# Kernel generation of a four-layer model: inverse deviations on ScalarE, the angle in turns, copies moved from VectorE, values and products exchanged in memory, another order of issue

## The chip, the cores and the metric

The kernel runs on one core of a Trainium2 chip. A core has TensorE (PE, matrix products; its weight loads are listed as PEld), VectorE (DVE, elementwise work and reductions), ScalarE (ACT, elementwise work, copies and functions from a table), GpSimd (POOL), and SyncE (SP), which here issues nearly all DMA transfers. Each engine takes its own instructions in the order in which they are written for it, and waits on semaphores for what other engines produce. The metric is the device time of one execution in microseconds (us).

## The reference, cut to what matters

The model is x = x + A(norm(x)), x = x + B(norm(x)), and both once more with the same weights. x has 2048 rows of 512 bf16 elements.

```
_layernorm: (x - mean) / sqrt(var + 1e-5)

A:  q, k, v = split(x @ wqkv), 32 heads of 16
    each position attends to itself and 7 earlier ones, 2 apart (pos, pos-2, ... pos-14)
    o = softmax(q.k * 16**-0.5, masked where the index is below 0) applied to v;  A = o @ wo

B:  dt = exp(log_dt);  K[d, l] = Re sum_n C[d,n] * exp(dt[d] * A[d,n] * l) * dt[d] * B[d,n],   l = 0 .. 2047
    y = causal convolution of u with K along the rows (by FFT) + u * Dskip
```

A, B and C are complex and given as real and imaginary parts, each 512 x 128. The convolution kernel K doesn't depend on x, so it is made once and serves both B layers.

## The kernel before, in words

There are five stages in time: the generation of K (0 to 117 us), attention layer 0 (to about 202), convolution layer 0 (to about 285), attention layer 1 (to about 378), convolution layer 1. The diff lies in the first, at the borders of the second, and in the order of two memory pools that both attention layers open.

**Generation of K** (`k_gen`, from L884). Its *head* is written out in L905 to L955. The parameters are loaded; PE turns each of them (`transposed`, L924); ACT makes dt = exp(log_dt) (L930); DVE forms dt\*A_im and dt\*A_re from the turned tiles (L939, L940), reduces the angle to one turn (L941 to L944); ACT takes exp of the real part, the sine, the absolute value and, from it, the cosine (L945 to L948); DVE multiplies (L954, L955). That is exp(dt\*A), the first power. Constants of the convolution come from `build_b_consts` (L574), which also hands back a list of small ACT steps (`steps`), a store (`w2_store`, 16 DMAs) and two DVE multiplications (`masks`).

Then powers are squared up eleven times (`square` on ACT, `double` and `differ` on DVE), copied by ACT to bf16 (`power`, `power_neg`), and one plane of each of five powers is duplicated by DMA (`power_copy`). From them DVE builds B_t, the powers for 21 lags (`b_part`), and four tables A_t, each for 32 channels, by doubling (`tables`: a copy of the head c_t at L1098, then five levels of products). PE multiplies tables by B_t (`product`, 16 times), ACT evacuates (`produced`), and `k_store` writes K to DRAM with 24 DMAs. All vector work of this kind shows as L983 in the profile, since one helper records it.

Between these instructions the *front* of attention layer 0 is woven in, for four blocks of 512 rows: load of x (`x_load`), statistics on ACT (`pass_stats`; block 3 by DVE), variance on DVE (`norms`, L1038 to L1055), the inverse deviation (`pow_`, L1059), normalization on ACT (`apply`, L158) or DVE (block 3, L160), turns on PE (L1068), their evacuation (L1071), the projections to keys and queries (L1078, L1083), and the halo copies: the keys of the last rows shifted by one partition (`front_ext`, L247), by DMA for blocks 0 to 2, and by DVE for block 3 (L255). Last come the first three logits products (`first_logits`) and their sums on PE (`la.lsum`).

The order of all this is a string, `ORDERK` (L44): each letter issues the next item of one list. s: square, i: double and differ, b: powers, c: power copies, C and M: c_part and b_part, G: the small ACT steps, g: masks, w: w2_store, a: statistics, l: norms, W: inverse deviation, y and z: normalization on ACT and on DVE, t and e: turn and evacuation, k, q and K, Q: projections and their evacuation, d: loads of x blocks 2 and 3, E: halo by DMA, T and U: tables 0, 2 and tables 1, 3, p and x: product and evacuation, X: first logits products (with the DVE halo before each), Z: their sums, 3: statistics of block 3. Each letter lands on one engine's queue, so the string fixes what stands behind what on every engine.

**Attention layer 0** (`LayerA.core`, L307). For each quarter q and part ft, DVE multiplies queries by eight shifted keys (`mult`, L295), PE sums over the head's 16 elements (`lsum`, L302), ACT takes exp. Projections to values (`v_proj`, L348, evacuated by ACT at L350) go between. After values 14 and 15 a DMA pair shifts values by a partition (L353, L354). Then DVE multiplies attention and values (`pv_mult`, L399), PE sums (L407) and projects (L419). `ev` is a table of further calls at given places: `("v", 1)` is after the second value shift, where all of x is loaded (`x_load`, L1318), `("m", 1, 0)` is ahead of the product of quarter 1, part 0.

Pools in SBUF lie over one another as they are opened: the generation's tiles are freed when its block ends, and the attention's pools take their place. A tile waits for the last reader of whatever lay there. `prp` holds the two product buffers (8 KB per partition each), `big` the values v_ext (30 KB) and the output weights (4 KB).

**Convolution layer 0** (`FftB.run`, with `ORDER0`, L50). Its `late` list holds five calls left over from the attention (the last rows' normalizations, on POOL), one of which is issued after each K letter from the second on.

Of the kernel before, what the change touches and what calls it, by code (L numbers as in the profile page):

```python
# [35 lines left out]
PI_LO = 3.1415920  # L36
# [8 lines left out]
iCsCGiCCCbbsiiMCaasMbiMiaMsCibbiMMaCsbcMTabaiTTibsMTiaMaciTTlbMTlcsiibblTsbTibcTWGiTlbsiGGMGTicM  # L45
GyiaMMMyyyabsGGTaaMGtMMatieMdGMTakaMMqMaMblMlaeaMlMMqkisWMMMaKiMQlywMyMqGyqyMbaMkktTtUQKUapUaUxk
apkKUUUqUxUUpUdUepa3UlTqUleQTkkkKTlUqxTkqK3TkQWqTxk3pTlTxT3yKTlpxpyTkyqkyptTlQkKUqkteqKeTUUTQkkk
WUTUxlkKkUkEKkzUzKpzUUqkEzUxpUKxtUUUUUetpqxekQUkkpxKUUkKkpUxEXkkxpUXKXxqpXXqXQgkpKZZZgxx
# [114 lines left out]
class LayerA:  # L163
# [143 lines left out]
    def core(self, x_sb, u, lnp, ev=None, nprod=0):  # L307
# [14 lines left out]
        with ExitStack() as c2:  # L322
            self.prp = c2.enter_context(tc.tile_pool(name=f"a{l}_prod", bufs=2, reuse_waits="tile"))
            big = c2.enter_context(tc.tile_pool(name=f"a{l}_big", bufs=1, reuse_waits="tile"))
# [3 lines left out]
            self.load_wo(big)  # L328
            wv, wo = self.wv, self.wo
# [15 lines left out]
            def v_proj(a):  # L345
# [5 lines left out]
                if a >= 14:  # L351
                    b = a - 14
                    nc.sync.dma_start(v[1:113, b:14:2, :], v[0:112, 16 + b:30:2, :])  # L353
                    nc.sync.dma_start(v[113:128, b:14:2, :], v[112:127, 16 + b:30:2, :])  # L354
                    event(("v", b))
# [57 lines left out]
            def out_proj(a):  # L413
# [4 lines left out]
                for ftp in range(NDT):  # L418
                    nc.tensor.matmul(pw[:], lhsT=oT[:, ftp, :], rhs=wo[:, ftp, :], start=False, stop=(ftp == NDT - 1))  # L419
# [112 lines left out]
            self.warm(pw, 10, wo[:, 0, :])  # L532
# [41 lines left out]
def build_b_consts(nc, cpool, tmp, w2_dram):  # L574
# [30 lines left out]
    def off_cols(name, rcol, v00, v10, v01, v11):  # L605
        o = tmp.tile([P, 2], F32, name=name)
        nc.vector.tensor_scalar(o[:, 0:1], rcol, float(v10 - v00), float(v00), ALU.mult, ALU.add)
        nc.vector.tensor_scalar(o[:, 1:2], rcol, float(v11 - v01), float(v01), ALU.mult, ALU.add)
        return o

    off = off_cols("w2_off", rik, 2048 * 8, 0, 4096 * 8, 2048 * 8)
    eo = tmp.tile([P, 1], F32, name="w2_eo")
    nc.vector.scalar_tensor_tensor(eo[:], ak, 512.0, d4k, ALU.mult, ALU.mult)
    nc.vector.tensor_tensor(off[:], off[:], eo[:].to_broadcast([P, 2]), ALU.add)
    wps = (("Wp", (4, 12, 0, 8)), ("WpJ", (8, 8, 4, 4)))
    wo = {name: off_cols("off_" + name, rim, *(4096 * o for o in offs)) for name, offs in wps}
    f1t = [tmp.tile([P, P], I32, name=f"f1_t{j}") for j in range(2)]
    qi = tmp.tile([P, EQ, 16, 2], I32, name="w2_qi")
    wt = {name: tmp.tile([P, 2, 16], I32, name="t_" + name) for name, offs in wps}
    ws, w2q = {}, {}  # L620
    sc = 2.0 * math.pi / 65536 * SIN_SHRINK

# [3 lines left out]
    def sine(o, i):  # L626
        nc.scalar.activation(o, i, ACT.Sin, scale=sc)

    def f1_sine(nm, t):
        C[nm] = cpool.tile([P, P], BF16, name=nm)  # L630
        sine(C[nm][:], low16(t[:]))

    def w2_sine():
        w2q[0] = tmp.tile([P, EQ, 32], BF16, name="w2_q", tag="w2_base")
        sine(w2q[0][:].rearrange("p e x -> p (e x)"), low16(qi[:].rearrange("p e m r -> p (e m r)")))

    def w_sine(name):
        ws[name] = cpool.tile([P, 32], F32, name="s_" + name)
        sine(ws[name][:], low16(wt[name][:].rearrange("p r a -> p (r a)")))

    def w_mask(name):
# [8 lines left out]
    def w2_store():  # L650
        for s in range(4):
            for j in range(4):
                nc.sync.dma_start(w2_dram[j::4, s * EQ:(s + 1) * EQ, j * 32:(j + 1) * 32], w2q[0][s::4])
# [787 lines left out]
```

## Time and profile before

| | |
|---|---|
| time, median of 4 runs | 435.51 us (433.08 to 436.96) |
| profiled execution, time | 433.53 us |
| profiled execution, span from first to last instruction | 431.7 us |
| DVE busy | 392.9 us (91%) |
| PE busy | 350.4 us (81%) |
| ACT busy | 322.2 us (75%) |
| POOL busy | 54.9 us (13%) |
| DVE's last product of the head starts | 11.27 us |
| first turn of an x block on PE | 41.52 us |
| product of quarter 0, part 3 starts | 117.26 us |
| first product of attention and values starts | 143.95 us |

The durations behind the steps below are those of one profiled execution. An engine's busy share says how much of the span it works, not whether it sets the end; the waits say who waited for whom, and the chain of work that ended last follows the time back from the last instruction. Names are those of the tiles without their numbers, so that all table work is "A_t" and all products of queries and keys are "prod", "A_pr" or "A2_pr".

### The profile page before, as it was taken

The numbers are of one execution on the slowest core, as the hardware profiler recorded it, in microseconds if no ns is written. First come the engines' busy times: TensorE is split into PE (matmuls) and PEld (weight loads), VectorE is DVE, ScalarE is ACT, GpSimd is POOL, SyncE is SP. The second block draws the span as 40 slices with busy tenths as digits, with TensorE's granted clock in tenths as the row PEclk, the third lists the DMA queues.
The fourth block names the chain that finished last, engine by engine and source line by source line (L and its number), as shares of the span: only waits on it lengthen the run. The fifth ranks groups of instructions, "written<-read, shape, count | busy, mean of one in ns | idle before, by whom it ended". The sixth has DMA issues, their size and how long they took to land.

```text
span 431.7 us, 12684 instructions
## 1 busy us (share of the span) xinstructions
PE 350.4 (81%) x5459; PEld 264.1 (61%) x5502; DVE 392.9 (91%) x549; ACT 322.2 (75%) x544; POOL 54.9 (13%) x46
## 2 busy tenths in 40 slices
PE   2000358998999889999887899999999899997795
PEld 2000117566755667777787798555567777777794
DVE  8999999999999999996989859879999999889874
ACT  6999968676465469987899997864556569689962
POOL 2004040260495000000500000000000020000000
PEclk9999998999999999999999999999999999999999
DMA  8931462132024555482165630860032066225305
GB/s 221 382 102 24 75 71 68 24 70 64 14 46 140 148 177 170 128 348 99 69 241 203 254 124 2 235 205 2 2 92 81 2 256 225 72 88 169 128 27 171
DMA packets 62467, 54.17 MB, mean 125 GB/s; under 512 B 33893, under 2 KB 50890, under 8 KB 61130
## 3 DMA queue, kind: packets, MB, share of 16 engines
q1 hardware_dynamic: 62266, 53.22, 39.9%
q8 instruction: 43, 0.70, 0.6%
q10 hardware_dynamic: 144, 0.13, 0.2%
q14 instruction: 14, 0.11, 0.1%
HBM read 30.28 MB, written 13.24 MB: 101 GB/s over the span
## 4 chain that ended last, share of the span: by engine, by line
PE 40%; DVE 18%; ACT 13%; DMA 5%; SPq 3%; issue 3%; POOL 2%; DVEq 0%; ACTq 0%; POOLq 0%
PE po L407 7%; DVE A_t L983 5%; PE pq L348 4%; DVE prod L295 4%; ACT a1s L726 4%; PE pq L419 4%; PE L L302 3%; PE pp L242 3%; PE pq L185 3%; PE pb L809 3%; PE pb L810 2%; DVE t L784 2%; DVE pav L399 2%; ACT ub L796 2%; PE pk L1135 2%
## 5 line engine op out<-in xcount | busy, mean ns | idle before, releaser
L399 DVE TENSOR_TENSOR pav<-attn,v_ext 128x4096 bf16<-128x4096 bf16 x32 | 72.7, 2281 | 0.0
L295 DVE TENSOR_TENSOR prod<-qT,kT_ext 128x4096 bf16<-128x4096 bf16 x29 | 66.3, 2304 | 0.2
L407 PEld LDWEIGHTS <-pav 128*128 128x128 bf16 x1024 | 58.7, 98 | 11.6 <-DVE pav L399 8.0
L407 PE MATMUL po<-ident,pav 128*128 128x128 bf16 x1024 | 62.5, 219 | 3.5 <-DVE pav L399 3.5
L1068 PE MATMUL pt<-ident,x_blk 128*128 128x128 bf16 x64 | 7.2, 260 | 40.0 <-ACT x_blk L158 38.7
L983 DVE TENSOR_TENSOR A_t<-A_t,pow_t 128x1024 bf16<-128x1024 bf16 (+4 forms) x46 | 38.2, 869 | 0.2
L796 ACT CAST ub<-pb 128x1024 bf16<-128x1024 f32 x32 | 33.0, 1089 | 2.2 <-DVE t L784 2.1
L1078 PE MATMUL pp<-xnT,kT_ext 128*128 128x512 bf16 x87 | 25.9, 421 | 10.7 <-ACT xnT L1071 8.3
L350 ACT CAST v_ext<-pq 128x512 bf16<-128x512 f32 x32 | 18.7, 586 | 20.4 <-PE pq L348 16.5
L809 PE MATMUL pb<-Wp,t 128*128 128x128 bf16 x256 | 30.1, 219 | 2.6 <-ACT ub L796 2.4
L302 PEld LDWEIGHTS <-prod 128*128 128x128 bf16 x928 | 27.0, 96 | 8.3 <-DVE prod L295 3.0
L744 PE MATMUL pb<-a1s,w_sb 128*128 128x64 bf16 x768 | 27.1, 193 | 5.7 <-ACT ub L796 3.5
L348 PE MATMUL pq<-wv,xnT 128*128 128x512 bf16 x118 | 30.2, 379 | 1.2 <-ACT v_ext L350 0.7
L1068 PEld LDWEIGHTS <-x_blk 128*128 128x128 bf16 x64 | 5.1, 116 | 42.6 <-ACT x_blk L158 40.8
L726 ACT CAST a1s<-pb 128x1024 bf16<-128x1024 f32 x30 | 29.3, 1077 | 1.3 <-PE pb L737 1.3
L410 ACT CAST oT<-po 128x512 bf16<-128x512 f32 x32 | 18.5, 579 | 15.7 <-PE po L407 15.6
L810 PE MATMUL pb<-WpJ,t 128*128 128x128 bf16 x256 | 30.1, 219 | 0.0
L419 PE MATMUL pq<-wop,oT 128*128 128x512 bf16 x110 | 29.3, 379 | 0.9
L744 PEld LDWEIGHTS <-w_sb 128*128 128x128 bf16 x768 | 24.7, 98 | 8.1 <-issue 7.0
L1059 POOL TENSOR_TENSOR ln_rstd<-ln_rstd,ln_mh 128x4 f32<-128x4 f32 x4 | 20.3, 5079 | 72.2 <-DVE ln_rstd L1054 49.2
L302 PE MATMUL L<-ind,prod 128*128 128x8 bf16 x928 | 27.5, 166 | 0.6 <-DVE prod L295 0.4
L726 DVE CAST a1s<-pb 128x1024 bf16<-128x1024 f32 x18 | 21.5, 1219 | 6.2 <-PE pb L737 5.9
(226 smaller groups left out, 873.3 us busy)
## 6 DMA issues: line engine op xcount, KB each, us to landing
w_sb<-w_dram SPq DMA_DIRECT2D x8, 1024.0 KB, 8.0
w_dram<-w_zero SPq DMA_DIRECT2D x1, 4096.0 KB, 14.5
kf_ring<-kf_dram SPq DMA_DIRECT2D x13, 256.0 KB, 3.7
kf_ring<-kf_dram SPq DMA_DIRECT2D x26, 128.0 KB, 3.6
v_ext<-v_ext SPq DMA_DIRECT2D x4, 784.0 KB, 6.1
x_blk<-in_A_x_dram SPq DMA_DIRECT2D x4, 512.0 KB
kT_ext<-in_A_wqkv_dram SPq DMA_DIRECT2D x4, 512.0 KB, 5.3
x_sb<-in_A_x_dram SPq DMA_DIRECT2D x4, 512.0 KB, 6.6
```

Source lines behind the costliest of these rows:

```text
L295: nc.vector.tensor_tensor(pr, self.qT[q][:, ft].unsqueeze(1).to_broadcast([P, W, 4, P]), kap, ALU.mult)
L302: self.nc.tensor.matmul(L[:, al, w, ft * 8:(ft + 1) * 8], lhsT=pr[:, w, al, :], rhs=self.c["ind8"][:], start=(ft == 0 and w == 0 and al % ...
L348: nc.tensor.matmul(pp[:], lhsT=xnT[:, dt, a * P:(a + 1) * P], rhs=wv[:, dt, :], start=(dt == 0), stop=(dt == NDT - 1))
L399: nc.vector.tensor_tensor(pv[:], attn[:, n % 4].unsqueeze(2).to_broadcast([P, W, DH, H]), vap, ALU.mult)
L407: nc.tensor.matmul(po[:, ft, :], lhsT=pvf[:, w, ft * P:(ft + 1) * P], rhs=ident[:], start=(w == 0 and ft == 0), stop=(w == W - 1), skip_gr ...
L419: nc.tensor.matmul(pw[:], lhsT=oT[:, ftp, :], rhs=wo[:, ftp, :], start=False, stop=(ftp == NDT - 1))
L726: (self.nc.scalar.copy if eng == "act" else self.nc.vector.tensor_copy)(dst, src)
L744: nc.tensor.matmul(p2[:, j, :], lhsT=self.w2[:, ec * EC + j, :], rhs=a1s[:, ec * EC + j, :], start=True, stop=True)
L796: nc.scalar.copy(ub[:], p2)
L809: nc.tensor.matmul(p3[:, j, :], lhsT=t1[:, dql, :], rhs=wp_r, start=True, stop=False)
L810: nc.tensor.matmul(p3[:, j, :], lhsT=t2[:, dql, :], rhs=wpj_r, start=False, stop=True)
L983: return lambda: nc.vector.tensor_tensor(*args)
```

## The change

1. *Head.* The loads of A_re and A_im change places. The angle is formed in turns: one DVE operation multiplies the turned A_im by 1/(2 pi) and dt, one adds the rounding constant, one takes it off and subtracts, one takes the larger of the turn and its negative. ACT's sine and cosine take 2 pi as their scale; ACT's absolute value, the clamp and one subtraction are gone. dt is written without reordering, and its readers reorder. Two memsets of B_t move from DVE to POOL, and what `build_b_consts` does with small offsets moves behind the angle (`rest`).
2. *Inverse deviations.* POOL's power and DVE's addition of the epsilon give way to ACT's Ln and Exp. The table set that holds both is loaded ahead of the first; the load in `ev` at `("m", 1, 0)` is gone.
3. *Table heads.* The copy of c_t is a letter of its own for tables 1 to 3 (H), on ACT.
4. *Halos.* Of block 3, parts 0 to 2 are copied by ACT (letter o).
5. *Masks.* They move from the end of the generation on DVE to POOL, as a sixth call of convolution layer 0's `late`.
6. *Memory.* `big` is opened ahead of `prp`, in both attention layers. In layer 0 the output weights are loaded after the first value shift, and x block 0 there too; x blocks 1 to 3 after the second.
7. *Order.* `ORDERK` is another string.

```diff
 ORDERK = """
-iCsCGiCCCbbsiiMCaasMbiMiaMsCibbiMMaCsbcMTabaiTTibsMTiaMaciTTlbMTlcsiibblTsbTibcTWGiTlbsiGGMGTicM
-GyiaMMMyyyabsGGTaaMGtMMatieMdGMTakaMMqMaMblMlaeaMlMMqkisWMMMaKiMQlywMyMqGyqyMbaMkktTtUQKUapUaUxk
-apkKUUUqUxUUpUdUepa3UlTqUleQTkkkKTlUqxTkqK3TkQWqTxk3pTlTxT3yKTlpxpyTkyqkyptTlQkKUqkteqKeTUUTQkkk
-WUTUxlkKkUkEKkzUzKpzUUqkEzUxpUKxtUUUUUetpqxekQUkkpxKUUkKkpUxEXkkxpUXKXxqpXXqXQgkpKZZZgxx
+sibCCiGCsiCbGCiMisibsbGcCiCMibabcsMMCMTMGiiMTGMaTbaisiTMbbcTTsiaTGbibsTTaiiaTbbbcMsTGaiGMaMMiGMb
+lMlaMGsGWiiaMalbMyyyyTMMaaiaMtMMweMtaMMMMedTaqcMMMslMkMaqlQkiqWKMbMqMlkyHyQTkyUkUkyKTtUqtKUUppaU
+qaUaUUqUxaUqaQakapxUelQekdUlpUkWKkKHxkqTlT3Tky3qxKTT3pT3pTQylyqxTkWqylxQpTkKtpzzTqzeTkqHtkxQeKUU
+zktkKkUEETkeUUktKTkkUkKTUUeKkkpkxpKUxkpUEUxUKkqUxUUUUpqoUkpoxKXUQxoUkpkKXZpxXxpxZZ
 """
...
         with ExitStack() as c2:
+            big = c2.enter_context(tc.tile_pool(name=f"a{l}_big", bufs=1, reuse_waits="tile"))
             self.prp = c2.enter_context(tc.tile_pool(name=f"a{l}_prod", bufs=2, reuse_waits="tile"))
-            big = c2.enter_context(tc.tile_pool(name=f"a{l}_big", bufs=1, reuse_waits="tile"))
...
-            self.load_wo(big)
-            wv, wo = self.wv, self.wo
+            wv = self.wv
+            if l:
+                self.load_wo(big)
...
                     nc.sync.dma_start(v[113:128, b:14:2, :], v[112:127, 16 + b:30:2, :])
+                    if b + l == 0:
+                        self.load_wo(big)
                     event(("v", b))
...
-            nc.vector.tensor_tensor(C[name][:], ws[name][:].unsqueeze(2).to_broadcast([P, 32, 4]),
-                                dmask_m.unsqueeze(1).to_broadcast([P, 32, 4]), ALU.mult)
+            nc.gpsimd.tensor_tensor(C[name][:], ws[name][:].unsqueeze(2).to_broadcast([P, 32, 4]),
+                                    dmask_m.unsqueeze(1).to_broadcast([P, 32, 4]), ALU.mult)
...
-        for name in ("A_im", "A_re", "B_re", "B_im", "C_re", "C_im"):
+        for name in ("A_re", "A_im", "B_re", "B_im", "C_re", "C_im"):
...
-        nc.vector.memset(Bt[:, 0, :, 0, :], 1.0)
-        nc.vector.memset(Bt[:, 1, :, 0, :], 0.0)
+        nc.gpsimd.memset(Bt[:, 0, :, 0, :], 1.0)
+        nc.gpsimd.memset(Bt[:, 1, :, 0, :], 0.0)
...
-        nc.scalar.activation(nat(dtb[:]), ldt[:].rearrange("p g q -> p q g"), ACT.Exp)
+        nc.scalar.activation(dtb[:], ldt[:].rearrange("p g q -> p (g q)"), ACT.Exp)
+        dtv = dtb[:].rearrange("p (g q) -> p q g", g=4)
...
-        nc.vector.tensor_tensor(nat(a_im), transposed("A_im"), nat(dtb[:]), ALU.mult)
-        nc.vector.tensor_tensor(nat(a_re), transposed("A_re"), nat(dtb[:]), ALU.mult)
-        nc.vector.tensor_scalar(t1[:], a_im, 1.0 / TWO_PI, MAGIC, ALU.mult, ALU.add)
-        nc.vector.tensor_scalar(t1[:], t1[:], MAGIC, None, ALU.subtract)
-        nc.vector.scalar_tensor_tensor(a_im, t1[:], -TWO_PI, a_im, ALU.mult, ALU.add)
-        nc.vector.tensor_scalar(a_im, a_im, PI_LO, -PI_LO, ALU.min, ALU.max)
+        nc.vector.tensor_tensor(nat(a_re), transposed("A_re"), dtv, ALU.mult)
         nc.scalar.activation(a_re, a_re, ACT.Exp)
-        nc.scalar.activation(sn, a_im, ACT.Sin, scale=-1.0)
-        nc.scalar.activation(t2[:], a_im, ACT.Abs)
-        nc.scalar.activation(cs, t2[:], ACT.Sin, bias=math.pi / 2 * (1 - 4e-7), scale=-1.0)
+        nc.vector.scalar_tensor_tensor(nat(turn), transposed("A_im"), 1.0 / TWO_PI, dtv, ALU.mult, ALU.mult)
+        nc.vector.tensor_scalar(t1[:], turn, MAGIC, None, ALU.add)
+        nc.vector.scalar_tensor_tensor(turn, t1[:], MAGIC, turn, ALU.subtract, ALU.subtract)
+        nc.vector.scalar_tensor_tensor(t2[:], turn, -1.0, turn, ALU.mult, ALU.max)
+        nc.scalar.activation(sn, turn, ACT.Sin, scale=TURN)
+        nc.scalar.activation(cs, t2[:], ACT.Sin, bias=math.pi / 2 * (1 - 4e-7), scale=-TURN)
+        steps, w2_store = rest()
...
-                yield lambda: nc.vector.tensor_scalar(rstd[:], var, EPS, None, ALU.add)
                 yield lambda: nc.vector.scalar_tensor_tensor(nb[:], mean, ms, rstd[:], ALU.mult, ALU.mult)
...
-        def pow_(b):
+        def inv_std(b):
             r = ln[b][0]
-            nc.gpsimd.tensor_tensor(r[:], r[:], lnst["mh"][:, 0:4], ALU.pow)
+            if b == 0:
+                nc.scalar.preload_act_table_set(EXP_LN)
+            nc.scalar.activation(r[:], lvar[b], ACT.Ln, bias=EPS)
+            nc.scalar.activation(r[:], r[:], ACT.Exp, scale=-0.5)
...
-            yield lambda: nc.vector.tensor_copy(A[:, :, :, 0, :], c0[:, :, c * CH * 4:(c + 1) * CH * 4].rearrange("p r (q g) -> p r q g", g=4))
+            (nc.scalar.copy if c else nc.vector.tensor_copy)(
+                A[:, :, :, 0, :], c0[:, :, c * CH * 4:(c + 1) * CH * 4].rearrange("p r (q g) -> p r q g", g=4))
...
             for ft in range(3):
-                yield lambda: la.front_ext(3, "dve", ft)
                 yield lambda: mult(ft)
...
-        ev = {("v", 1): [x_load], ("o", 1): [lambda: k_half_load(0)], ("o", 2): [G(gs, 0)], 
-              ("m", 1, 0): [lambda: nc.scalar.preload_act_table_set(EXP_LN)],
+        ev = {("v", 0): [lambda: x_load((0,))], ("v", 1): [lambda: x_load((1, 2, 3))], ("o", 1): [lambda: k_half_load(0)], ("o", 2): [G(gs, 0)], 
...
         late = la.core(x_sb, u, lnp, ev, 3)
+    late.append(C["masks"])
```

## The prediction

> **What bounds the kernel now.** I read the per-engine totals first, then busy time by stretch, then the waits, the chain that ended last, and the timeline of the stretch that the diff touches. Nearly all of the diff lies in the first of five stages, the generation of the convolution kernel. The table by stretch (engine busy time of each stretch, clock, DMA share, GB/s):
>
> ```profile
> 12.00:40.00 28.00, 0.00 (x0) 0.00 (x0) 27.06 (x50) 27.15 (x44) 4.86 (x1) 1.00 0.52 179
> 40.00:70.00 30.00, 14.19 (x80) 7.76 (x83) 28.92 (x48) 25.74 (x56) 5.07 (x1) 0.94 0.43 62
> 70.00:96.00 26.00, 24.64 (x323) 16.68 (x326) 25.14 (x41) 19.71 (x33) 10.32 (x2) 1.00 0.23 54
> 96.00:115.00 19.00, 17.21 (x296) 13.45 (x299) 18.66 (x27) 10.91 (x17) 1.23 (x4) 1.00 0.16 40
> 115.00:135.00 20.00, 19.04 (x290) 11.50 (x293) 19.84 (x16) 10.51 (x18) 20.00 (x14) 1.00 0.23 55
> ...
> 160.00:185.00 25.00, 24.59 (x352) 19.35 (x354) 24.59 (x24) 23.29 (x48) 1.01 (x1) 1.00 0.53 160
> ```
>
> The columns after the length are PE, PEld, DVE, ACT, POOL. From 12 us to 185 us VectorE (DVE) is 96 to 99% busy, through the generation (to 117 us) and the first attention layer (to 190). So a DVE microsecond saved in the generation is worth one, until another engine ends last. Where DVE is idle (the waits, total, times, longest):
>
> ```profile
> DVE ln_nb L1055 <- POOL ln_rstd L1059: 2.7, 3, 0.9
> DVE sq_z L954 <- ACT ws L946: 0.7, 1, 0.7
> DVE sq_z L955 <- ACT ws L948: 0.5, 1, 0.5
> ```
>
> and the chain that ended last passes the third of these POOL waits into TensorE:
>
> ```profile
> 88.78 7.31 POOL ln_rstd L1059
> ...
> 99.50 0.90 PE pt L1068 x13
> ```
>
> Four numbers per partition raised to -0.5 take 7.31 us on GpSimd; then DVE normalizes block 3, PE turns it and has no gap worth a word until 117. The stretch ends so on DVE, ACT and PE:
>
> ```profile
> 116.07 0.28 DVE L643 TENSOR_TENSOR Wp<-s_Wp,aux 128x128 bf16<-128x128 f32 x1
> 116.28 0.69 DVE L643 TENSOR_TENSOR WpJ<-s_WpJ,aux 128x128 bf16<-128x128 f32 x1
> 116.89 0.28 DVE L255 COPY kT_ext<-kT_ext 128x508 bf16<-128x508 bf16 x1
> 117.26 4.72 DVE L295 TENSOR_TENSOR prod<-qT,kT_ext 128x4096 bf16<-128x4096 bf16 x2
> ```
> ```profile
> 118.10 1.07 ACT L350 CAST v_ext<-pq 128x512 bf16<-128x512 f32 x2 [3.62 <-PE L L302]
> ```
> ```profile
> 117.07 0.94 PE L302 MATMUL L<-ind,A_pr 128*128 128x8 bf16 x32
> ```
>
> The first value eviction waits 3.62 us for the third logits sum, because its tile lies over that product's buffer.
>
> **What the Trainium skill says.** "SBUF — State Buffer", section "SBUF: two separate sides": DVE and GpSimd share a port pair under an exclusive lock. The trace agrees: the same 4-element power takes 3.09 to 7.30 us beside a full DVE, 1.01 us once at 174. "ScalarE: Activation LUTs", "What ACT_TABLE_LOAD costs": 1283 ns plus a drain of 1380. The trace has the 1.28 us (at 8.10) but the next activation starts 0.05 after it, so I price 1.3. "Table sets: the hidden batching unit" of the same page: exp and ln lie in one set; at 121 to 131 us one load serves Exp, Ln, Exp, so it agrees. The first of these sections also prices an ACT copy at 186 ns + 0.833 per element, 93 overlapped: 0.31 us for 256 elements, 0.52 for 508 (estimates; 512-element copies here follow at 0.48).
>
> **The change, part by part** (start-to-start times, since DVE instructions overlap by some 0.08).
>
> *Head.* DVE ends it at 11.27 + 0.69 = 11.96. After: eight small w2 offset operations (4.75 to 5.46) and two B_t memsets (5.52 to 6.28) no longer stand ahead of the first product. It can start when the first transpose, done at 5.55, is seen: 5.65, not 6.19. It is now the A_re product, so its Exp ends by 6.95 and the Sin table by 8.25. The angle in turns costs DVE 0.60 + 0.45 + 0.70 + 0.65 to 8.6, the turn itself ready at 7.95. Sine 8.25 to 8.8, cosine 8.8 to 9.4, with no ACT Abs (0.61) between and no clamp (0.43). DVE has meanwhile done the eight offsets (0.6), and its two last products end at 9.75 and 10.4. Gain 1.55; bounds 0.8 (memsets on POOL delaying DVE) to 1.8.
>
> *Off DVE.* Four rstd adds (L1054) at 0.07: 0.28. Three table head copies (L1098) 0.27 + 0.13 + 0.14 = 0.54. Three halo copies (L255, parts 0 to 2) 0.20 + 0.32 + 0.37 = 0.89. Two masks, 116.07 to 116.89: 0.82. Sum 2.53. The masks go to GpSimd behind its last normalizations in the convolution stage, where POOL works 6.0 of 40 us and the inverse products need them some 30 us later: nothing, or about 1 us if that cover is gone.
>
> *The POOL waits* at 38.6, 61.8 and 95.2: 0.91 + 0.91 + 0.90 = 2.72, gone. In their place ACT does Ln and Exp, 0.19 + 0.21 seen at 187.7, with a handover to and from DVE, and DVE has 0.6 to 2 us of other products ordered in between. One table load (1.28) comes before the first; the load at 121.26 goes, where ACT idles half the time, so neither ends last.
>
> *New order.* I laid both order strings out and added each letter's duration along its queue. DVE carries 101.8 us before and 99.5 after, ACT 83.8 and 88.9, PE 48.6 twice. Check on before: 12.0 + 101.8 + 2.7 = 116.5, seen 116.9. ACT after ends near 10.4 + 88.9 = 99.3 plus waits, eleven short of DVE, so it can't bound the sum, only single steps. The tightest: the 16 w2 stores, 11.48 us of SP issue, now stand ahead of the load of x block 2 and of the fifth power copy. They can start when their sine is done (some 30 us of ACT work: 40.7), end at 52.2, the load goes at 52.6 (before 45.88), just when its buffer is free, and lands about 56.5. ACT reaches its statistics at 57.2. The copy lands by 57, its reader comes at 62. Cost 0.4, bounds 0 and 3.
>
> *Value pool below the products.* Summing tile sizes from the bottom, the product buffers leave the power tables (free early) and now lie over the second and third first-logits products; values lie over the first two. So value evictions wait for the second sum, not the third, and the product of part 3 waits for the third sum. Queued behind it on DVE is all of the attention; PE waits for that. The product ends, the sum takes 0.94, DVE has only 0.28 of its own: 0.85 of wait if PE is up to date, 1.8 if it is 1.0 late as at 117.07, none if the buffer falls elsewhere. I take 1.0. The output weights' four loads (3.3 us of SP) move behind the first value shift, and x block 0 ahead of the second: SP idled 137.0 to 144.0 there, so the 4.2 us hide; uncovered they would delay the second shift by at most that. PE's 0.6 wait for x_sb at 152 goes, DVE never saw it.
>
> **Sum.** 1.55 + 2.53 + 2.72 = 6.8 saved, 1.0 + 0.4 given back: **5.4 us**. Attention follows DVE without a gap to 190, and later stages follow attention, so it carries. Span 431.7 becomes 426.3, the profiled execution 433.53 becomes 428.1. The median of the runs shown is 2.0 above that execution, so I forecast 435.51 - 5.4 = **430.1**.
>
> **Rivals.** (a) *Handovers take the place of the POOL waits*: ACT gained 5.1 us of work, in a string where DVE and ACT run within a microsecond of each other up to the 50th microsecond of work, and half of that lands on DVE. For it: squares, powers, table heads and Ln/Exp now all share ACT's queue. Against: ACT idles for 17 of 105 us. 435.5 - 2.8 = 432.7. (b) *Nothing is given back*: 435.5 - 6.8 = 428.7; the buffer falls elsewhere and x arrives in time. (c) *Slower, by SP order*: the w2 stores write 64-byte rows and hold the DMA engines at 0.62 to 0.81; if block 2 lands behind them 14 us after issue, ACT stalls about 10, and through the second inverse deviation DVE loses about 8.6: 438.7. It turns the result from a landing at 63.5 on. Against it: the stores themselves landed 2.7 to 3.5 us after issue, and the x load took 3.5.
>
> **Chances.** About 1% (4.4 us) is what a measurement can tell from no change. Forecast and (b) together, gains above 4.4: 0.61. (a), gains of 0 to 4.4: 0.30. (c) 0.09, of which 0.02 end within 1%. Faster 0.61, same 0.32, slower 0.07. The low end is (b) less the 2 us by which single runs fall around their median, 426.7, the high end no gain at all, 435.5, with half a microsecond on it.
>
> **What would show it.** DVE's two head products end near 10.4. No wait of DVE for POOL before 170, and ACT's Ln/Exp without a wait of DVE over 0.3 behind them. The fourth product of the first tile starts at about 112, preceded by about 1 us of waiting for L; the first pav at about 138.5 (143.95). After that the same gaps as before. I am wrong if DVE waits for ACT in 40 to 80 us, if the statistics of block 2 wait for their load, or if the attention, starting earlier, ends later than 5 us before 202.

## The result and the profile after

The changed kernel takes 432.67 us (median of 34 runs, 430.21 to 435.76) where the kernel before, run beside it, takes 435.00 (53 runs, 433.08 to 438.00). The ratio is 0.9948, with a 95% interval of 0.9933 to 0.9962: a gain of 2.3 us, clear of noise, but less than half of the 5.4 that were forecast. The profiled execution took 432.41 us, its span is 430.6, only 1.1 below that of before. Up to the first convolution stage it is 2.55 ahead, at 320 us 2.98, at 381 us 1.50. The granted clock was 0.83 from 330 to 340 us, where before has 1.00, and 0.3 is lost there; of the rest, lost between 354 and 381 us at a clock of 1.00 in both, 0.6 is a wait of DVE for ACT's rs at 360 us, and what remains is not explained.

| start of | before | forecast | after |
|---|---|---|---|
| end of DVE's last product of the head | 11.96 | 10.4 | 11.85 |
| end of the third first-logits product | 116.07 | | 112.42 |
| fourth product of the first tile | 117.26 | 112 | 114.94 |
| its wait for the sum L | none | 1.0 | 2.07 |
| first product of attention and values (pav) | 143.95 | 138.5 | 141.40 |
| third pav | 151.69 | | 149.14 |
| DVE's first evacuation of the convolution stage | 203.42 | | 200.87 |

The gain is there at the fourth product (2.32 us) and stays through the first attention layer: what decides it lies before 115 us. The table by stretch of the kernel after (PE, PEld, DVE, ACT, POOL busy, clock, DMA share, GB/s):

```profile
12.00:40.00 28.00, 0.00 (x0) 0.00 (x0) 28.00 (x47) 26.61 (x43) 0.00 (x0) 1.00 0.52 177
40.00:70.00 30.00, 14.79 (x117) 8.25 (x120) 29.74 (x50) 28.98 (x62) 3.79 (x2) 1.00 0.45 72
70.00:96.00 26.00, 24.16 (x305) 16.22 (x309) 25.93 (x44) 23.72 (x44) 0.00 (x0) 1.00 0.24 50
96.00:115.00 19.00, 17.80 (x352) 14.29 (x353) 16.79 (x18) 10.52 (x17) 3.36 (x6) 1.00 0.18 43
115.00:135.00 20.00, 18.66 (x253) 10.53 (x254) 19.93 (x13) 9.48 (x17) 17.72 (x11) 1.00 0.34 83
```

Up to 96 us DVE has 0.33 us of idle time in 84 (before: 2.9). The POOL waits are gone and nothing has come in their place. In the fourth stretch it idles 2.2 of 19. DVE's waits name the new one, and the one at the head:

```profile
DVE prod L295 <- PE L L302: 2.1, 1, 2.1
...
DVE sq_z L947 <- PE pt L933: 0.6, 1, 0.6
```

The timeline of DVE (start, length, what; in brackets the idle time ahead of it) at the head, and where the attention begins:

```profile
5.92 1.03 DVE L947 TENSOR_TENSOR sq_z<-pt,dt_bf 128x512 f32<-128x512 bf16 x1 [0.62 <-PE pt L933]
6.87 1.04 DVE L949 SCALAR_TENSOR_TENSOR ws<-pt,dt_bf 128x512 f32<-128x512 bf16 x1
...
11.16 0.69 DVE L962 TENSOR_TENSOR sq_z<-sq_z,ws 128x512 f32<-128x512 f32 x1
...
112.42 0.45 DVE L255 COPY kT_ext<-kT_ext 128x508 bf16<-128x508 bf16 x1
114.94 4.49 DVE L295 TENSOR_TENSOR prod<-qT,kT_ext 128x4096 bf16<-128x4096 bf16 x2 [2.07 <-PE L L302]
```

The two products with dt take 1.03 and 1.04 us; before, they took 0.63 and 0.68, with the same tile sizes and types:

```profile
6.19 0.63 DVE L939 TENSOR_TENSOR ws<-pt,dt_bf 128x512 f32<-128x512 bf16 x1
6.74 0.68 DVE L940 TENSOR_TENSOR sq_z<-pt,dt_bf 128x512 f32<-128x512 bf16 x1
```

And PE's timeline where the attention begins:

```profile
111.36 0.96 PE L302 MATMUL L<-ind,A_pr 128*128 128x8 bf16 x32
112.23 1.89 PE L349 MATMUL pq<-wv,xnT 128*128 128x512 bf16 x7
113.96 0.94 PE L302 MATMUL L<-ind,A_pr 128*128 128x8 bf16 x32
```

and before:

```profile
114.53 0.82 PE L348 MATMUL pq<-wv,xnT 128*128 128x512 bf16 x2
115.19 0.94 PE L302 MATMUL L<-ind,A_pr 128*128 128x8 bf16 x32
116.00 1.24 PE L348 MATMUL pq<-wv,xnT 128*128 128x512 bf16 x5
```

The third product ends at 112.42, but its sum starts at 113.96: PE is in value projections, which lie between the second and the third sum. Before, three such matmuls lay ahead of the second sum and five ahead of the third (the trace lacks the record of one of the three, and here that of one of eight), and that sum started 1.0 after its product's end (117.07 and 116.07); here all eight lie ahead of the third, and it is 1.54 late. The string doesn't show this: in both strings the second and the third sum stand side by side (ZZ), and the attention issues the value projections later; in both traces they run between the sums.

### The profile page after: what moved, and what is told of

Same layout as the page of the kernel before. It is cut to its first block, busy times and chain, and to the rows that moved or that the text cites. A ratio compares the mean times of both kernels' runs of the same rounds, so it can differ in the third digit from the quotient of the medians.

```text
span 430.6 us, 12686 instructions
## 1 busy us (share of the span) xinstructions
PE 349.6 (81%) x5459; PEld 263.9 (61%) x5502; DVE 392.1 (91%) x534; ACT 325.9 (76%) x557; POOL 39.1 (9%) x46
## 4 chain that ended last, share of the span: by engine, by line
PE 46%; DVE 16%; ACT 13%; DMA 4%; issue 4%; SPq 1%; ACTq 0%; DVEq 0%
PE po L410 8%; DVE prod L295 5%; PE pk L1150 5%; DVE pav L402 5%; ACT a1s L733 4%; PE pq L349 4%; PE pq L422 4%; PE pp L1088 4%; PE L L302 3%; PE pp L242 3%; PE pq L185 3%; PE pb L816 3%; PE pb L817 2%; ACT ub L803 2%; DVE t L791 2%
## 5 line engine op out<-in xcount | busy, mean ns | idle before, releaser
L410 PEld LDWEIGHTS <-pav 128*128 128x128 bf16 x1024 | 60.2, 99 | 12.0 <-DVE pav L402 8.1
L410 PE MATMUL po<-ident,pav 128*128 128x128 bf16 x1024 | 64.0, 222 | 4.1 <-DVE pav L402 4.0
L1078 PE MATMUL pt<-ident,x_blk 128*128 128x128 bf16 x64 | 6.3, 241 | 43.4 <-ACT x_blk L158 43.4
L817 PEld LDWEIGHTS <-t 128*128 128x128 bf16 x256 | 25.0, 98 | 3.0 <-issue 1.9
```

The costliest lines, as they stand in the source:

```text
L410: nc.tensor.matmul(po[:, ft, :], lhsT=pvf[:, w, ft * P:(ft + 1) * P], rhs=ident[:], start=(w == 0 and ft == 0), stop=(w == W - 1), skip_gr ...
L817: nc.tensor.matmul(p3[:, j, :], lhsT=t2[:, dql, :], rhs=wpj_r, start=False, stop=True)
```

## The experiments

All times are medians of 6 to 34 executions (six in experiments 1, 5, 6, 8 and 11), each beside runs of the kernel before on the same chip. "Fourth product" and "third pav" are the places of the table above, "head ends" is the end of DVE's last product of the head; these three are from one trace each. With the new head, this end scatters from trace to trace: PE's first transpose, which waits for the load of A_re, starts at 4.89 to 5.20 in the ten traces that have this head, and DVE's first product of the head at 5.62 to 5.92. The kernel after has the latest of the ten, so up to 0.3 us of a difference to it is not the work of the edit. In experiment 2, where the edit doesn't touch the head, it starts so:

```profile
5.65 1.03 DVE L950 TENSOR_TENSOR sq_z<-pt,dt_bf 128x512 f32<-128x512 bf16 x1 [0.35 <-PE pt L936]
```

| edit | time, ratio (95% interval) | head ends | fourth product | third pav |
|---|---|---|---|---|
| after | 432.67, 0.9948 (0.9933, 0.9962) | 11.85 | 114.94 | 149.14 |
| after, dt in natural order | 431.62, 0.9902 (0.9866, 0.9939) | 11.04 | 113.42 | 147.62 |
| after, pools of layer 0 as before | 432.72, 0.9934 (0.9910, 0.9959) | 11.57 | 112.77 | 148.62 |
| after, products moved up by a pad | 432.80, 0.9933 (0.9912, 0.9955) | 11.73 | 112.83 | 148.38 |
| after, power on POOL again | 436.79, 1.0029 (1.0002, 1.0057) | 11.73 | 119.37 | 153.58 |
| after, dt and pad | 430.82, 0.9895 (0.9850, 0.9940) | 11.12 | 111.83 | 147.38 |
| after, old order | 443.83, 1.0191 (1.0147, 1.0235) | 11.55 | 126.05 | 162.36 |
| after, copies on DVE again | 434.42, 0.9974 (0.9956, 0.9992) | 11.54 | 115.17 | 149.38 |
| before, inverse deviations on ACT | 444.53, 1.0198 (1.0151, 1.0245) | 11.97 | 121.16 | 161.68 |
| after, old order, common table named | 437.02, 1.0066 (1.0042, 1.0090) | 11.59 | 119.46 | 153.85 |
| before, the same, common table named | 435.85, 1.0015 (0.9998, 1.0031) | 11.97 | 117.85 | 152.86 |
| after, dt and pad, index work on ACT | 428.92, 0.9873 (0.9839, 0.9907) | 10.87 | 111.40 | 145.09 |
| before, pools exchanged | 435.35, 1.0015 (0.9996, 1.0033) | 11.97 | 118.08 | 152.28 |

**1. dt in natural order.** ACT's exponential writes dt in the order of its readers again, as before the change.

```diff
-        nc.scalar.activation(dtb[:], ldt[:].rearrange("p g q -> p (g q)"), ACT.Exp)
-        dtv = dtb[:].rearrange("p (g q) -> p q g", g=4)
+        nc.scalar.activation(nat(dtb[:]), ldt[:].rearrange("p g q -> p q g"), ACT.Exp)
+        dtv = nat(dtb[:])
...
-                yield tt(nat(c0[:, q]), nat(cb), dtv, ALU.mult)
+                yield tt(c0[:, q], cb, dtb[:], ALU.mult)
```

> The changed kernel with dt stored as before: ScalarE writes it reordered, so that its four readers on VectorE read it in sequence (the two products of the head, the two c_t products). Theory A (the new layout of dt made each of the four 0.36 to 0.41 us longer: 1.03 and 1.04 for 0.63 and 0.68 in the head, 1.04 for 0.69 at c_t): all four fall back to 0.63 to 0.69, dt itself takes 1.07 on ScalarE instead of 0.63 but is ready at about 5.65, before the first product at 5.92; the fourth product of the first tile starts 1.4 us earlier, at about 113.5, and the time is 1.4 us below that of the changed kernel, about 431.2 (ratio to before 0.9915). Rival B (the head is set by ScalarE's table load and sines, or the generation's end by TensorE): the products are shorter, the end moves by less than 0.5 us (ratio 0.994 to 0.995).

The products fall to 0.69 and 0.68, the head ends at 11.04, and the fourth product and the attention behind it come 1.52 us earlier, 0.10 of it because the head's first product starts sooner:

```profile
5.82 0.69 DVE L947 TENSOR_TENSOR sq_z<-pt,dt_bf 128x512 f32<-128x512 bf16 x1 [0.87 <-PE pt L933]
```

By the ratios the time is 2.0 us below that of the changed kernel, but the intervals overlap; the trace decides, for A. DVE's group of the two c_t products, of the kernel after and of this one:

```profile
L990 DVE TENSOR_TENSOR c_t<-ws,dt_bf 128x512 bf16<-128x512 f32 x2 | 2.1, 1044 | 0.0
```
```profile
L990 DVE TENSOR_TENSOR c_t<-ws,dt_bf 128x512 bf16<-128x512 f32 x2 | 1.4, 684 | 0.0
```

So four DVE instructions paid 0.35 us each for reading dt at a stride of 256 bytes. ACT's exponential, which reordered in their place, takes 1.08 us against 0.63, and DVE waits for PE's first transpose in either case: the 0.45 that ACT saved shortened nothing.

**2. Pools of layer 0 as before**: products below the values again, in layer 0 alone.

```diff
+            if not l:
+                self.prp = c2.enter_context(tc.tile_pool(name=f"a{l}_prod", bufs=2, reuse_waits="tile"))
             big = c2.enter_context(tc.tile_pool(name=f"a{l}_big", bufs=1, reuse_waits="tile"))
-            self.prp = c2.enter_context(tc.tile_pool(name=f"a{l}_prod", bufs=2, reuse_waits="tile"))
+            if l:
+                self.prp = c2.enter_context(tc.tile_pool(name=f"a{l}_prod", bufs=2, reuse_waits="tile"))
```

> The changed kernel with the product buffers below the values again, in attention layer 0 alone. Theory A (the 2.07 us wait of the fourth product for the third logits sum is a pure loss, VectorE sets the end): the wait is gone, that product starts at about 112.9 and all that follows comes 2.0 us earlier, about 430.7 (ratio 0.990). Rival B (behind it stands the chain of the values: value evictions now wait for the third sum at 114.9 instead of the second at 112.3, the second value shift, which landed at 148.1 ahead of the third attention product at 149.1, comes later): the product starts at 112.9, but the third attention product waits for the shift and starts no earlier than 148.5; gain 0 to 0.6 us (ratio 0.993 to 0.995).

The wait for L is gone and the fourth product comes 2.17 us earlier, 0.28 of it from the earlier head. But the value evictions now wait for the third sum, PE waits for them, the next reduction waits for L:

```profile
115.33 1.89 PE L352 MATMUL pq<-wv,xnT 128*128 128x512 bf16 x8 [0.72 <-ACT v_ext L354]
118.49 1.23 DVE L366 TENSOR_REDUCE mx<-L 128x128 bf16<-128x1024 f32 x1 [1.02 <-PE L L285]
```

At the third pav 0.52 is left, 0.24 without the head. B by its numbers, but not by its shift: the third pav doesn't wait; the time is lost ahead of it.

**3. A pad**: values stay at the bottom, and the products lie behind the small tiles and a pad of 2.25 KB, clear of the third first-logits product (layer 0 alone).

```diff
             big = c2.enter_context(tc.tile_pool(name=f"a{l}_big", bufs=1, reuse_waits="tile"))
-            self.prp = c2.enter_context(...)
+            if l:
+                self.prp = c2.enter_context(...)
...
             wk = c2.enter_context(tc.tile_pool(name=f"a{l}_wk", bufs=2, reuse_waits="tile"))
+            if not l:
+                pad = c2.enter_context(tc.tile_pool(name="a0_pad", bufs=1, reuse_waits="tile"))
+                pad.tile([P, 1152], BF16, name="pad")
+                self.prp = c2.enter_context(...)
```

> The changed kernel with the product buffers of attention layer 0 opened above the small work tiles and 2.3 KB of padding, so that they lie over a table of the last products (read to 111.3) and over no first-logits product; the values stay where the change put them. Theory A (VectorE sets the end): no wait for the third sum, the fourth product at about 112.9, everything 2.0 us earlier, about 430.7 (ratio 0.990). Rival B (value chain): value evictions are as early as in the changed kernel, so the shift lands at about 148.1 as there and the third attention product can't start before about 148.2: gain 0.9 us at most, about 431.8 (ratio 0.992 to 0.993).

Now neither waits, yet of 2.11 us at the fourth product 0.76 are left at the third pav (0.64 without the earlier head), and nothing sure is seen in the time (by the ratios 0.65 us, with intervals that overlap). The gain is B's, but again no pav waits for the shift. The timelines show where the rest goes. POOL makes index tables (L683, L684 of the kernel after) from 111 us on. In the kernel after, two of its eight multiplications fall into DVE's 2.07 us of idle time and take 1.39 us:

```profile
112.70 1.39 POOL L684 TENSOR_SCALAR g_i<-g_i,aux 128x512 int32<-128x512 int32 x2
...
115.11 5.47 POOL L684 TENSOR_SCALAR g_i<-g_i,aux 128x512 int32<-128x512 int32 x2
```

and with the pad:

```profile
112.58 5.53 POOL L689 TENSOR_SCALAR g_i<-g_i,aux 128x512 int32<-128x512 int32 x2
112.83 4.80 DVE L295 TENSOR_TENSOR prod<-qT,kT_ext 128x4096 bf16<-128x4096 bf16 x2
136.07 0.83 DVE L384 TENSOR_TENSOR s<-ex 128x512 bf16<-128x512 bf16 x1
```

With the pad DVE is busy there, each pair takes 5.3 to 5.6, POOL ends at 137.46 instead of 132.72, and beside it DVE's product takes 4.80 for 4.49 and the second tile's sums 0.83 and 0.66 for 0.41 and 0.29. The idle time had paid for POOL's work; without it, DVE pays (experiment 11 takes that work away). The prediction cited the lock on the shared port (the Trainium skill, "SBUF — State Buffer", section "SBUF: two separate sides") for a power that DVE lengthens; by that section, when a DVE operation with two SBUF inputs meets a GpSimd one that reads SBUF, whichever starts first blocks the other. Here DVE's instructions lengthen, by 0.31 to 0.42 us, which agrees in kind; no run tells the lock from another cause.

**4. The power on POOL again**, with DVE's addition of the epsilon, at the new places.

```diff
-            nc.scalar.activation(r[:], lvar[b], ACT.Ln, bias=EPS)
-            nc.scalar.activation(r[:], r[:], ACT.Exp, scale=-0.5)
+            nc.vector.tensor_scalar(r[:], lvar[b], EPS, None, ALU.add)
+            nc.gpsimd.tensor_tensor(r[:], r[:], lnst["mh"][:, 0:4], ALU.pow)
```

> The changed kernel with the inverse deviations on GpSimd again (VectorE adds the epsilon where the letter W stands, GpSimd raises to -0.5). Theory A (a GpSimd power ends only once VectorE stops, so each costs VectorE a wait of about 0.9 us as the three in the kernel before, plus 0.07 for the addition): four waits, the fourth product of the first tile 3.5 to 4 us later than in the changed kernel, about 118.7, time about 436.4 (ratio 1.003). Rival B (the waits were covered elsewhere, other engines were late anyway): less than 1.5 us later (ratio below 0.998).

```profile
DVE ln_nb L1062 <- POOL ln_rstd L1069: 3.6, 4, 1.2
...
DVE A_t L990 <- ACT A_t L1109: 0.3, 1, 0.3
```

A: the waits are back, four of them, and 4.43 us at the fourth product (4.55 without the earlier head). 3.6 + 0.3 of waits and 0.3 of additions account for 4.2 of it. In this order, taking the power off POOL is worth its waits in full.

**5. dt and pad together.**

> The changed kernel with both mends at once: dt written in the natural order again, and in layer 0 the value pool at the bottom but the product buffers moved up by a pad, clear of the third first-logits product. Theory A (both losses are on VectorE's path and add): the fourth product starts at about 111.4, with no wait for L of more than 0.3; the third pav at about 146.9 (147.6 with dt alone, less 0.76 that the pad alone gave); time 0.8 us below dt alone, 430.8. Theory B (GpSimd's index generation, which sits beside VectorE from 111 us on, takes the pad's gain back, as with the pad alone): the fourth product at 111.4 too, but VectorE's short sums before attn and the products beside GpSimd grow by 1.5 us or more in all, the third pav at 147.3 or later, time as with dt alone, 431.6.

The fourth product is at 111.83, the third pav at 147.38, 0.24 before that of dt alone: by the trace most of the pad's gain is taken back as in experiment 3 (product 4.80, sums 0.83 and 0.66, and a halo copy of 0.69 for 0.45). The time, 430.82, is 0.8 below dt alone, as A has it, but the ratios differ by 0.0007 and their intervals overlap; the trace decides, for B.

**6. The new kernel in the old order.** The order string of before, without its two mask letters and its four epsilon letters; table heads and halos on ACT stand where DVE's copies stood.

> The changed kernel with the order string of before (its mask letters and its four epsilon letters left out, each moved table head and halo copy at the place where it stood). Theory A (the new order moves VectorE little by itself, the POOL waits went because the power left GpSimd): VectorE waits for ScalarE at Ln/Exp or at table heads by less than 1 us in all, the fourth product at 114 to 116, time within 1 us of the changed kernel, 431.7 to 433.7. Theory B (ScalarE has 5 us more in front of VectorE, and the old order has no room for it): VectorE waits for ScalarE by 2 to 5 us in all between 12 and 112 us, the fourth product at 117 or later, time 434.5 or more.

By the ratios 10.6 us slower than the new order, far past B. DVE waits 3.0 for a table head and 2.3 for Ln and Exp before 112 us, then 3.2 for the halo copy and 3.4 for L. ACT's timeline shows a cause that neither theory named:

```profile
96.57 1.28 ACT L1068 ACT_TABLE_LOAD   x1
97.86 0.20 ACT L1068 ACTIVATE ln_rstd<-ln_ag 128x4 f32<-128x4 f32 x1
98.09 1.28 ACT L1069 ACT_TABLE_LOAD   x1
99.38 0.20 ACT L1069 ACTIVATE ln_rstd<-ln_rstd 128x4 f32<-128x4 f32 x1
```

In the whole run ACT loads 19 tables, where before and after load 5. The kernel names the set that has both Exp and Ln once, ahead of the first inverse deviation. In the old order sines come after that (at 48.77 and 66.72 us); they load their own table, and from then on each Ln and each Exp loads one of its own, in the attention of layer 0 too (six loads, beside L384 and L386). The Trainium skill, "ScalarE: Activation LUTs", section "Table sets: the hidden batching unit", counts Ln and then Exp as one load, since one set has both. Here that held only where that set was already the active one.

**7. Copies on DVE again**: table heads 1 to 3 and the three halos; the masks too, at their new, late place.

```diff
-            (nc.scalar.copy if c else nc.vector.tensor_copy)(
+            nc.vector.tensor_copy(
...
-            nc.gpsimd.tensor_tensor(C[name][:], ws[name]...
+            nc.vector.tensor_tensor(C[name][:], ws[name]...
...
-... o=calls(lambda ft: la.front_ext(3, "act", ft), (0,), (1,), (2,)) ...
+... o=calls(lambda ft: la.front_ext(3, "dve", ft), (0,), (1,), (2,)) ...
```

> The changed kernel with table heads and halo copies back on VectorE (and the two masks on VectorE at their new, late place). Theory A (what leaves VectorE in the generation shortens the run by its own length): 0.54 + 0.89 = 1.43 us later at the fourth product, 116.4, the wait for L stays at 2.1, time 434.1. Theory B (the wait for L absorbs it, since it ends by TensorE's value projections, which don't depend on these copies): the wait shrinks to 0.6 to 1.0, the fourth product within 0.4 of 114.94, time as the changed kernel, 432.7 within 0.5.

```profile
115.17 4.49 DVE L295 TENSOR_TENSOR prod<-qT,kT_ext 128x4096 bf16<-128x4096 bf16 x2 [1.50 <-PE L L302]
```

The third product ends 0.97 later, the wait shrinks by 0.57, and the fourth product is 0.23 later; without the earlier head of this execution (0.31) it would be some 0.54. So B's mechanism is there, the wait ends by PE's queue and takes up part of the copies, but less of them than B has it. The time is A's (434.42; by the ratios 1.1 us above the changed kernel), in part for another reason: the masks on DVE at 207 us (0.71 and 0.28) delay the convolution stage by another 0.8, from 0.56 at its start to 1.34 at 233 us.

**8. The kernel before with the inverse deviations on ACT**, and nothing else.

```diff
-                yield lambda: nc.vector.tensor_scalar(rstd[:], var, EPS, None, ALU.add)
+                lvar[b] = var
+                yield lambda: None
...
-            nc.gpsimd.tensor_tensor(r[:], r[:], lnst["mh"][:, 0:4], ALU.pow)
+            if b == 0:
+                nc.scalar.preload_act_table_set(EXP_LN)
+            nc.scalar.activation(r[:], lvar[b], ACT.Ln, bias=EPS)
+            nc.scalar.activation(r[:], r[:], ACT.Exp, scale=-0.5)
...
-              ("m", 1, 0): [lambda: nc.scalar.preload_act_table_set(EXP_LN)],
```

> The kernel before with only the inverse deviations moved: Ln and Exp on ScalarE in the place of VectorE's epsilon add and GpSimd's power, the order string as it was. Theory A (the forecast's terms): the three POOL waits, 2.72, and four adds, 0.28, go: the fourth product at 114.3 (117.26 before), time 3.0 us below before, ratio 0.993. Theory B (handovers take their place): VectorE waits for ScalarE's Ln/Exp by half of that, the fourth product at 115.7 or later, ratio 0.9965 or more.

By the ratio 8.6 us slower instead of 3.0 faster, with the same 19 loads: both theories fall. 3.9 us are lost by the fourth product, the rest beside it and in the attention (mx waits 3.6 for L, attn 2.9 for rs).

**9 and 10. The same two, with the common table named ahead of the first three inverse deviations.**

```diff
-            if b == 0:
+            if b < 3:
                 nc.scalar.preload_act_table_set(EXP_LN)
```

> The changed kernel with the order of before, as in the run with the old order, but the table that holds both exp and ln is named ahead of the first three inverse deviations, not the first alone: the Sin activations that the old order has between them no longer leave Ln and Exp with a table each. Theory A (the old order cost 11 us because every Ln and Exp, in the generation and in the first attention layer, loaded its own table): table loads fall from 20 to about 10 in the whole run, none is left beside the attention's Ln and Exp, VectorE's waits for rs go, time 436 or less. Theory B (the order itself is what is missing, ScalarE is too late for halo copies and value evictions): VectorE still waits about 3 us for the halo copy and 3 us for L, time 438.5 or more.

> The kernel before with the inverse deviations on ScalarE, as in the run that moved them alone, with the same naming of the common table ahead of the first three. Theory A (the forecast's price of the POOL waits, 3.0 us, holds once tables are not split; two table loads more than in the changed kernel cost ScalarE 2.6 us, half of it seen by VectorE): time 1 to 3 us below before, ratio 0.993 to 0.998. Theory B (without an order that has all sines first, the inverse deviations on ScalarE don't pay): ratio 1.000 or more, VectorE waiting for ScalarE or TensorE by 3 us or more between 12 and 125 us.

Loads fall to 9, none is left at the Ln and Exp of the attention. By the ratios that gives back 5.4 us in the new kernel (9) and 8.0 in the kernel before (10), which then ties with what it was. DVE's waits of the second:

```profile
DVE A_t L1102 <- ACT B_t L974: 2.1, 1, 2.1
DVE B_t L983 <- ACT B_t L974: 0.9, 1, 0.9
...
DVE ln_nb L1056 <- ACT ln_rstd L1063: 0.4, 2, 0.2
```

The POOL waits (2.7) are gone, and DVE waits 3.0 for powers that ACT copies: ACT, which was 27.15 us busy of 28 between 12 and 40 us in the kernel before, has four table loads more and the eight Ln and Exp. That these are what makes it late is the likely reading; no run takes them away singly. B holds for 10, its ratio being above 1.000. For 9, at 437.02, neither bound is met; of the waits that B named, the one for L is there (2.6), that for the halo is not. Its largest wait is another, 3.0 for a table head that ACT copies. So of the 10.6 us between the new and the old order of the new kernel, 5.4 went with ten table loads; in the other 5.2 are the four loads that it still has more than the new order, and the places of the rest, which no run separates.

**11. Index work on ACT.** The version with dt and pad; POOL's eight multiplications become ACT activations, at four places of the first tiles.

```diff
-            nc.gpsimd.tensor_scalar(g, g, p21, bias, ALU.mult, ALU.add)
+            nc.scalar.activation(g, g, ACT.Identity, scale=p21, bias=bias)
...
-              ("m", 0, 3): [G(gx, h) for h in range(4)],
+              ("m", 0, 3): [G(gx, 0)], ("m", 1, 0): [G(gx, 1)], ("m", 1, 2): [G(gx, 2)], ("m", 2, 0): [G(gx, 3)],
```

> The kernel with both mends (dt in natural order, product buffers moved up by a pad) and, further, GpSimd's eight index multiplications of 111 to 137 us as ScalarE activations, spread over four places in the first attention tiles; the index patterns stay on GpSimd. Theory A (GpSimd beside VectorE cost VectorE 0.3 to 0.4 us for each such instruction, about 2.3 us in all, as the lengthened products and short sums show): each prod takes 2.25, the short sums 0.41, 0.29, 0.29, the third pav starts 1.5 us earlier or more, at 145.9 or before, time 429.3. Theory B (ScalarE's 5 us more delay the value evictions, so the shifted values come later and the third pav waits for them, or a sum waits for TensorE): the third pav at 147.4 or later, time 430.8 or more.

```profile
111.40 4.50 DVE L295 TENSOR_TENSOR prod<-qT,kT_ext 128x4096 bf16<-128x4096 bf16 x2
...
121.91 0.42 DVE L384 TENSOR_TENSOR s<-ex 128x512 bf16<-128x512 bf16 x1
122.36 0.29 DVE L386 TENSOR_TENSOR s<-s 128x256 bf16<-128x256 bf16 x1
...
145.09 2.29 DVE L407 TENSOR_TENSOR pav<-attn,v_ext 128x4096 bf16<-128x4096 bf16 x1
```

A, throughout: products and sums have their usual lengths, the third pav comes 2.29 us earlier than in experiment 5 (2.04 without the earlier head), and 428.92 us is the lowest median, 1.3% below the kernel before. Its interval overlaps those of experiments 1 and 5; that the index work makes the difference is read from the trace. On ACT a pair of the multiplications takes 1.33.

**12. The kernel before with the pools exchanged.**

```diff
-            self.prp = c2.enter_context(tc.tile_pool(name=f"a{l}_prod", bufs=2, reuse_waits="tile"))
             big = c2.enter_context(tc.tile_pool(name=f"a{l}_big", bufs=1, reuse_waits="tile"))
+            self.prp = c2.enter_context(tc.tile_pool(name=f"a{l}_prod", bufs=2, reuse_waits="tile"))
```

> The kernel before with the two pools of the attention swapped and nothing else: values below the products. Theory A (the forecast's step: the fourth product now waits for the third sum, price 1.0): the fourth product at 118.2 (117.26 before), preceded by a wait of about 1 us for L, the value evictions ahead of it about 1 us earlier; time 436.5, ratio 1.002. Theory B (the wait moves from ScalarE's value eviction to VectorE and what is earlier in the values pays it back): third pav at the same time as before, ratio within 0.001 of 1. Theory C (the price in the changed kernel, 2.07, is that of the placement, whatever the queue): fourth product at 119.3, ratio 1.005.

```profile
118.08 4.49 DVE L295 TENSOR_TENSOR prod<-qT,kT_ext 128x4096 bf16<-128x4096 bf16 x2 [0.88 <-PE L L302]
```

A by its numbers: a wait of 0.88, 0.82 later at the fourth product, 0.59 at the third pav, and value evictions that no longer wait for the third sum (PE goes on at 117.90 instead of 118.73). But the match with the forecast's 1.0 is a coincidence. Here DVE still has the two masks, 0.82, between the third product and the fourth; without them, as in the changed kernel, the same PE queue would make it 1.7 (an estimate, 0.88 + 0.82), which is the forecast's late case (1.8).

## Why the prediction was wrong

It forecast 5.4 us and 2.3 came; the sign and the place were right. At the fourth product the forecast has 5.4, the trace 2.32. The shortfall of 3.1 splits by steps: the first three below make 3.23, the fourth gave 0.23 more than forecast, and 0.1 is the halo copy beside POOL (0.45 for 0.28, less a gap of 0.09 that closed).

- **Head: failed, by 1.44.** Gain 0.11, not 1.55, which is below the lower bound given (0.8). The step priced the products with dt from rows of before (0.68) and didn't ask in which layout they would read dt: the diff's "its readers reorder" moved a cost from ACT, which had slack, to DVE, which had none. Experiment 1 gives 0.71 of the 1.44 back in these two products. Another 0.27 is this execution's late start, 5.92 for 5.65; in five of the ten traces it is at 5.62 to 5.66, where the step had it. The bound that it named, the memsets on POOL, isn't the reason: beside them a DVE copy takes 0.62 instead of 0.17 in seven of the ten traces, and four of these seven have the early start. The last 0.46, still there in experiment 1, are distances between DVE's starts that the step took too short, most at the turn (0.71 for 0.60) and the sine's product (0.78 for 0.55).
- **The same layout outside the head: missed, 0.72.** The two c_t products (1.044 for 0.684) stood in the diff, and no step costed them.
- **Value pool below the products: mechanism right, term mis-sized, 2.07 for 1.0.** The wait is where the step put it and for what it said. It priced 0.85 with PE up to date and 1.8 with PE 1.0 late, as the profile of before had it, and took 1.0: it leaned to the end for which nothing in the profile spoke. Experiment 12 gives an estimate of 1.7 for PE's queue of before (0.88 and the masks' 0.82), and in the changed kernel eight value matmuls ahead of the third sum make PE 1.54 late. What put them there is not shown; it isn't the new order alone, since with the old order (experiment 9) that sum starts 1.90 after its product's end (118.48 and 116.58). But the 1.07 too much isn't worth 1.07 of time: removing the wait whole, by two routes, left 0.52 and 0.76 at the third pav (0.24 and 0.64 without the earlier heads), and nothing sure in the time (experiments 2, 3), since in the one the values come later and in the other POOL's index work lengthens DVE's instructions.
- **POOL waits and off DVE: right in sum.** From the head's end to the end of the third product DVE gained 3.54, and 0.72 was lost there to c_t: 4.26, where the terms (2.72 waits, 0.28 additions, 0.54 heads, 0.89 halos, less 0.4 for the order) give 4.03. The masks' 0.82 behind it went in full. They didn't run where the step saw them, in the convolution stage, but at 44.63 us, since POOL's order is not laid down by the string; no DVE wait came of it. Single terms are not additive, though: with the new wait for L behind them, heads and halos, 1.43 by the terms, are worth 0.23 to 0.54 at the fourth product (experiment 7, with and without its earlier head).
- **New order: wrong in kind.** It was priced as a cost of 0.4 beside the gain of the POOL waits. It is that gain's condition: without it the same edits end 10.6 us later (experiment 6), and the inverse deviations alone make the kernel before 8.6 us slower (experiment 8), or no faster with the tables mended (10). The step's "one table load comes before the first" was true because the order has all sines ahead of it. The rival of late SP work did not come: x block 2 was loaded at 54.19, for 52.6 in the step, and no engine waited for it.

The rival (a), gains of 0 to 4.4 us, named the right size and the wrong cause: no handover replaced the POOL waits (the list of DVE's waits has none for Ln and Exp). That its 432.7 is the measured time is luck. With the layout mended and the pad, the kernel gains 4.6 us (0.9895; 2.6 to 6.5 by the interval), which is near the forecast.

## What to carry to other kernels

When a diff takes a reordering out of one engine's write, look for who reads that tile, and price each reader with its stride; a saving on an engine with slack can be a loss on the one without. When a function moves to ScalarE, read the order for what table is active at that point, and ask it again for every later function of the set. And a wait can be paying for something: before removing it, look at what runs in that gap on the engine that shares memory access with the waiting one.

## What the hardware showed that was not expected

- DVE, 128 x 512 elements, one bf16 operand in SBUF read at a stride of 256 bytes: 1.03 to 1.05 us; read in order 0.68 to 0.69. In the head's two products the other operand was read at the same kind of stride from PSUM (the turned tile) in both cases, and with dt in order they take 0.68 to 0.69, no more than the c_t product, which reads no such tile (0.684).
- A pair of int32 multiplications of 128 x 512 on POOL: 1.39 us while DVE idles, 4.7 to 5.6 beside a busy DVE. Beside such a pair DVE's short sums take 0.83 and 0.66 for 0.41 and 0.29, a product of 2.28 takes 2.7.
- A table load takes 1.28 us, and the activation behind it starts within 0.02 us of its end, at each of the loads shown.
